# Thirteen full-array products first, and a head's half-column products kept together, in a fused attention and gated-MLP kernel

## The chip, the cores and the metric

The kernel runs on one core of a Trainium2 chip. What counts is the device time of one execution in microseconds (us). Five engines work side by side: TensorE (PE: matrix products, and the loading of their stationary operand, PEld), VectorE (DVE), ScalarE (ACT), GpSimd (POOL), and SyncE (SP), which issues the transfers.

## The reference

Eight batches of eight heads go through attention with a causal mask and a learned decay; the result, with the heads side by side as 512 features, goes through a gated MLP with a spatial product over the 576 tokens. Cut to what matters:

```python
scores = scale * np.matmul(q, k.transpose(0, 1, 3, 2))          # 64 heads, 576 x 576, D = 64
cum = np.cumsum(np.maximum(s, 0.0), axis=-1)
scores = np.where(causal, -1e9, scores + np.minimum(-(cum[..., :, None] - cum[..., None, :]), 0.0))
attn = softmax(scores)
x = (attn @ v) as (batch, 576, 512)

h = gelu(x @ w_in)                                              # 512 -> 1024, tanh form
u, v = h[..., :512], h[..., 512:]
v_n = (v - mean) / sqrt(var + 1e-6) * g_ln
out = x + (u * (w_sg @ v_n + b_sg)) @ w_out                     # w_sg is 576 x 576
```

## The kernel before

All activations lie feature-major. Per head the score matrix is worked in five row tiles (`IT0`, `ITR`, `ITW`): four of 128 query rows, which need 192, 320, 448 and 576 key columns, and one of 64 rows (`it` 0) that needs 64. Scores are products into PSUM (`sc`). DVE adds the mask, takes the row minimum of the negated scores and writes `p`; ACT takes the exponential with its row sum. TensorE transposes `p` block by block into `pt`, and ACT and DVE copy that to `pa`, `pb` and `pd`. Then `pv` forms the weighted sum in the PSUM tile `xx`. The row sums of a pair of heads are transposed once (`pt<-ident,rs`), sent out and read back as a row (`rb`), and POOL multiplies them in.

Three kinds of heads differ in precision. Heads 0 to 11 (`h < NQ`) take their scores from plain fp32 products of `kf` (64 features and one row of the cumulated decay). Heads 0 to 15 (`h < NP`) take the weighted sum in fp32 too. Every other product is a sum of products of rounded halves (fp32r: a high and a low part). One fp32 product is two instructions in the trace, one fp32r product is one.

In fp32 the weighted sum of a head is ten products (`part(side, ...)`): the stationary operand is a block of `v` with 64 columns, and `side` says which 64 of the 128 columns of the array, so which half of `xx`, it goes to. Side 1 sums the output columns 256 to 511, side 0 the others. The last two have 64 rows, since the last 64 keys are a half block.

After every eight heads follows the MLP of a batch: `v_unit` (`vm`), `u_unit` (`um`), `s_unit` (`sm`) and `o_unit` (`om`), all fp32r. Its weights are fetched (`wraw`), taken apart and rounded (`wbits`, `wm`, `wi`, `wo`, `ws`) by ACT, DVE and POOL during the first heads.

The order on each engine isn't that of the code. Each step carries a place in a timetable (`POS`, `spread`), in heads; `SHIFT` moves kinds of instructions by parts of it in five phases, and `plan` lists the instructions by a cost for each and by these priorities. The order it finds is then fixed. The `yield`s in `pv` let other work be placed between the pieces.

At the start the cumulated decay is a product of the decay rows with a triangle of ones (`cps<-tri,sp`), which waits for a transfer and for POOL and DVE, and `WARM` = 2 further products (`wm`) of the same operands follow it, whose result nobody reads. Head 0 has no decay row in `kf` yet, and adds it by products of a single row (`sc<-cf,tri`). Nearly all instructions are recorded at the line of one helper (L404).

Of the kernel before, what the change touches and what calls it, by code (L numbers as in the profile page):

```python
# [9 lines left out]
F32 = mybir.dt.float32  # L10
F32R = mybir.dt.float32r
# [6 lines left out]
B, H, S, D = 8, 8, 576, 64  # L18
# [3 lines left out]
P = 128  # L22
NC = DM // P
NT = 4
REM = S - NT * P
# [10 lines left out]
IT0 = [512, 0, 384, 128, 256]  # L36
COL = [4, 0, 3, 1, 2]
ITR = [64, 128, 128, 128, 128]
# [9 lines left out]
WARM = 2  # L48
FULL = {(128, 192): 300.0, (128, 288): 525.0, (128, 320): 690.0, (128, 448): 830.0, (64, 64): 130.0,
        (64, 128): 150.0, (64, 192): 215.0, (64, 256): 290.0}  # L50
NQ = 12
NP = 16
# [19 lines left out]
MARGIN = 33.09  # L72
# [3 lines left out]
    "act activation p__ 128x192 p__": (0, -1.37, 0, 0, 0),  # L76
    "act activation p__ 128x320 p__": (-2.28, -2.28, -2.28, -2.28, -2.28),
    "act activation p__ 64x64 p__": (2.65, 0, -4.17, 0, 0),
# [3 lines left out]
    "act copy k 128x576 raw": (0, 0, 6.86, 6.86, 6.86),  # L82
    "act copy pah 128x512 pt": (3.74, 3.74, 3.74, 3.74, 3.74),
    "act copy pbh 128x256 pt": (0, 2.82, 1.23, 0, 0),
    "act copy vs 128x384 vr": (0, 0, 0, 5.9, 0),
    "act copy wi 128x256 wbits": (1.22, 1.22, 1.22, 0, 0),
    "act copy wo 128x256 wbits": (0, 0, -0.77, -0.77, 0),
# [8 lines left out]
    "dve scalar_tensor_tensor wbits 128x256 wraw": (0, 0.25, 4.43, 0, 0),  # L96
    "dve scalar_tensor_tensor wm 128x256 wraw": (0, -5.7, 0, 0, 0),
    "dve tensor_copy pbl 128x512 pt": (0, 0, -2.8, 0, 0),
    "dve tensor_copy pdh 128x256 pt": (-3.99, -3.99, -3.99, -3.99, 0),
    "dve tensor_scalar wm 128x256 wbits": (1.21, 1.21, 1.21, 0, 0),  # L100
    "dve tensor_tensor pdh 64x64 pt": (0, 0, 0, 2.01, 2.01),
    "dve tensor_tensor xr 64x64 x": (0, 0, 0, 5.88, 5.88),
    "dve tensor_tensor_reduce p__ 128x192 sc": (-3.17, -3.17, -3.17, -3.17, -3.17),
    "dve tensor_tensor_reduce p__ 128x288 sc": (0, 0.71, 4.68, 0, 0),
    "dve tensor_tensor_reduce p__ 128x320 sc": (4.12, 0.53, 8.43, 1.82, 0),
    "dve tensor_tensor_reduce p__ 64x64 sc": (-9.27, -9.27, -9.27, -9.27, -9.27),
# [18 lines left out]
    "pool tensor_scalar wbits 128x256 wbits": (-4.38, -4.38, -4.38, -4.38, 0),  # L125
    "pool tensor_tensor k 128x576 raw": (0, 0, -8.31, -8.31, -8.31),
    "pool tensor_tensor wo 128x256 wbits": (0, 0, 19.21, 19.21, 0),
    "pool tensor_tensor ws 128x576 wst": (0, 0, -3.49, 0, 0),
# [109 lines left out]
class Program:  # L238
# [14 lines left out]


# [9 lines left out]
    def cost(self, op):  # L264
        e, name, ins, outs, kw = op["eng"].n, op["name"], op["ins"], op["outs"], op["kw"]
        big = [v for v in ins if v.columns() > 1]
        n = outs[0].columns() if outs else big[0].columns()
# [3 lines left out]
        if e == PE:  # L271
            if name == "transpose":
                d, load, port = 110.0, 0.84 * ins[0].columns(), 1.0
            else:
                w, m = ins
                load, n = 0.84 * w.columns(), m.columns()
                d = 0.463 * n if m.dtype == F32R else FULL.get((w.columns(), n), 2.0 * n + 60)
# [116 lines left out]
    def emit(self, tc, first, uses, order, text):  # L394


        real, todo = {}, {}
        for bs in uses:
            for b in bs:
                todo[b] = todo.get(b, 0) + 1  # L400
        for i in text:
            op = self.ops[i]
            f = lambda x: x.make() if isinstance(x, View) else x
            r = getattr(op["eng"].real, op["name"])(*[f(a) for a in op["args"]], **{k: f(v) for k, v in op["kw"].items()})  # L404
            real[i] = r.ins
            for b in uses[i]:
                todo[b] -= 1
                if todo[b] == 0:
                    b.real = None

        tags, same = {}, set()
        for i in text:
            for b in first[i]:
                tags.setdefault(b.tag, []).append(i)
        edges = [(a, b, mybir.DependencyClass.NoSync) for seq in order for a, b in zip(seq, seq[1:])]
        edges += [(a, b, mybir.DependencyClass.NoSync) for seq in tags.values() for a, b in zip(seq, seq[1:])
                  if self.ops[a]["eng"].n != self.ops[b]["eng"].n]
        for a, b, kind in edges:
            tc.add_manual_dep(real[b], real[a].name, mybir.DependencyInfo(kind, mybir.DependencyReason.DATA),
                              reason="order")  # L420
# [129 lines left out]
def tile_attn_gmlp(  # L550
# [45 lines left out]
    def load(h):  # L596
        d = heads[h] = {}
        if h < NQ:
            t = att.tile([P, 2, S], F32, name="kf", tag="k1")
            k, q = d["k"], d["q"] = t[0:D + 1, 0, :], t[0:D + 1, 1, :]  # L600
# [20 lines left out]
    cum = dram.tile([2, BH, S], F32, name="cum")  # L621
    st = moe.tile([P, 5, BH], F32, name="st", tag="vt", bufs=2)
# [21 lines left out]
    wm = ps_m.tile([P, 512], F32, name="wm", tag="m")  # L644
    for i in range(WARM):
        nc.tensor.matmul(wm, sp[:, 0].rearrange("p a h -> p (a h)"), tri[:, 0:512], start=True, stop=True)
# [134 lines left out]
    def qk_part(h, it, pst, c0, j0, j1):  # L781
        d = heads[h]
        i0, r = IT0[it], ITR[it]
# [148 lines left out]
    def pv(h):  # L932
# [20 lines left out]
        if f32:  # L953
            v, pa, pb, pd = d["v"], pt["pa"][0], pt["pb"][0], pt["pd"][0]

            def part(side, c0, c1, w, m, start=False, stop=False):
                nc.tensor.matmul(xx[64 * side:64 * side + 64, c0:c1], w, m, start=start, stop=stop)

            part(1, 256, 512, v[:, 0, :], pa[:, 256:512], start=True)
            part(0, 0, 256, v[:, 0, :], pa[:, 0:256], start=True)  # L960
            yield 0.2
            part(1, 256, 512, v[:, 1, :], pb[:, 512:768])
            part(0, 64, 256, v[:, 1, :], pb[:, 320:512])
            part(1, 256, 448, v[:, 2, :], pb[:, 128:320])
            part(0, 128, 256, v[:, 2, :], pb[:, 0:128])
            yield 0.65
            part(1, 256, 384, v[:, 3, :], pd[:, 192:320])
            part(0, 192, 256, v[:, 3, :], pd[:, 128:192])
            part(1, 256, 320, v[REM:P, 4, :], pd[REM:P, 64:128], stop=True)
            part(0, 256, 320, v[0:REM, 5, :], pd[0:REM, 64:128], stop=True)  # L970
# [237 lines left out]
def _layout(i):  # L1208
# [7 lines left out]
    kf = kq[:NQ].reshape(NQ, 2, D, S).transpose(0, 2, 1, 3)  # L1216
    kf = np.concatenate([kf, np.ones((NQ, 1, 2, S), q.dtype)], axis=1)
    v6 = np.concatenate([v, v[:, NT * P:], v[:, 0:REM], v[:, 0:REM]], axis=1)
    s_t = np.concatenate([i["s"].reshape(BH, S).T, np.zeros((5 * P - S, BH), i["s"].dtype)])
# [36 lines left out]
```

## Time and profile before

| | us |
|---|---|
| median of the runs | 795.68 |
| time of the profiled execution | 795.8 |
| span of its trace | 794.1 |
| TensorE busy | 782.0 (98%) |
| VectorE / ScalarE / GpSimd busy | 599.1 / 562.6 / 488.0 |

The span reaches from the first to the last instruction; 1.7 us of the execution's own time lie around it. The time of the engine that is always busy sets the end; of such an engine one then asks at which pace it works.

### The profile page before, as it was taken

To read this page: it belongs to the slowest core of one execution; us is meant where nothing else is said; L and a number is where in the kernel's file an instruction comes from. 1 tells how busy PE (TensorE), PEld (TensorE's weight loads), DVE (VectorE), ACT (ScalarE), POOL (GpSimd) and SP (SyncE) were. 2 spreads that over 40 slices of the span, in tenths; PEclk is the share of its full clock that TensorE was granted. 3 is DMA by queue.
4 is the path that set the end of the run, shared out by engine and by line. 5 is a ranking of instruction groups with operands and counts; after the bars stand their busy time and mean duration, and the time that the engine had idled before them with its cause. 6 is when DMAs were issued, how large, how long until landed. Compare 5 with 4: busy or idle time off the path is not lost.

```text
span 794.1 us, 16905 instructions
## 1 busy us (share of the span) xinstructions
PE 782.0 (98%) x5271; PEld 692.7 (87%) x5271; DVE 599.1 (75%) x1829; ACT 562.6 (71%) x1550; POOL 488.0 (61%) x762
## 2 busy tenths in 40 slices
PE   7999999999999999999999999999999999999998
PEld 4556667889989999999989999999989999999998
DVE  3477869867699868987799868987689867984562
ACT  2467777866689858987689857987689957972440
POOL 4245779774756766586655856576555856653641
PEclk9999999999999999999999999999999999999999
DMA  6246674545353635356353545355354544411101
GB/s 177 77 113 151 168 205 129 126 103 153 92 144 93 159 104 152 89 141 179 95 133 101 152 119 150 98 133 159 97 133 117 148 134 121 112 33 39 51 7 61
DMA packets 74115, 94.23 MB, mean 119 GB/s; under 512 B 29813, under 2 KB 44597, under 8 KB 74026
## 3 DMA queue, kind: packets, MB, share of 16 engines
q1 hardware_dynamic: 74026, 93.16, 44.4%
q8 instruction: 42, 0.69, 0.4%
q14 instruction: 47, 0.39, 0.2%
HBM read 49.38 MB, written 9.90 MB: 75 GB/s over the span
## 4 chain that ended last, share of the span: by engine, by line
PE 93%; DVE 2%; DMA 2%; ACT 2%; POOL 0%; issue 0%; SPq 0%; ACTq 0%
PE sc L404 16%; PE sm L404 14%; PE om L404 13%; PE um L404 13%; PE xx L404 13%; PE vm L404 12%; PE pt L404 11%; DMA wraw<-in_w_out 1%; ACT p L404 1%; DMA kf<-in_kf 0%; DVE wbits L404 0%; DVE p L404 0%; DMA k<-k 0%; PE cps L404 0%; PE x L404 0%
## 5 line engine op out<-in xcount | busy, mean ns | idle before, releaser
L404 ACT ACTIVATE p<-p,mn 64x64 f32<-64x64 f32 (+4 forms) x320 | 177.8, 556 | 58.9 <-DVE mn L404 56.9
L404 DVE CUSTOM_DVE_ANT_0 p<-sc,mask 128x448 f32<-128x448 f32 (+4 forms) x320 | 123.8, 421 | 24.1 <-PE sc L404 22.6
L404 PE MATMUL sm<-ws,vn 128*128 128x288 f32 x768 | 134.8, 300 | 0.0
L404 PE MATMUL pt<-ident,p 128*128 128x128 f32 x768 | 132.4, 280 | 1.0 <-ACT p L404 0.7
L404 PE MATMUL om<-gt,wo 128*128 128x288 f32 x768 | 129.8, 301 | 0.0
L404 PE MATMUL um<-xs,wi 128*128 128x288 f32 x768 | 127.0, 303 | 0.4 <-DVE vt L404 0.3
L404 PE MATMUL vm<-wi,xs 128*128 128x512 f32 (+1 forms) x416 | 117.6, 404 | 0.0
L404 PEld LDWEIGHTS pt<-ident,p 128*128 128x128 f32 x768 | 93.4, 142 | 23.8 <-issue 11.1
L404 PEld LDWEIGHTS sm<-ws,vn 128*128 128x128 f32 x768 | 112.6, 188 | 1.2 <-issue 0.3
L404 PEld LDWEIGHTS om<-gt,wo 128*128 128x128 f32 x768 | 110.6, 188 | 1.7 <-issue 0.3
L404 PEld LDWEIGHTS um<-xs,wi 128*128 128x128 f32 x768 | 107.6, 188 | 3.3 <-issue 0.8
L404 POOL TENSOR_TENSOR k<-raw,k 128x576 fp32r<-128x576 f32 x52 | 74.7, 1437 | 32.4 <-ACT k L404 30.9
L404 PE MATMUL sc<-k 128*128 128x288 f32 (+4 forms) x312 | 91.2, 304 | 0.0
L404 PE MATMUL sc<-k,q 66*128 66x288 f32 (+4 forms) x312 | 86.8, 307 | 0.0
L404 PEld LDWEIGHTS vm<-wi,xs 128*128 128x128 f32 (+1 forms) x416 | 73.2, 184 | 13.9 <-issue 1.0
L404 POOL TENSOR_SCALAR p<-p 64x64 f32<-64x64 f32 x128 | 30.9, 241 | 81.0 <-ACT p L404 50.5
L404 DVE TENSOR_TENSOR pbl<-pt,pbh 128x512 fp32r<-128x512 f32 x96 | 52.0, 547 | 23.1 <-ACT pbh L404 20.2
L404 POOL TENSOR_TENSOR gt<-u,gt 128x288 fp32r<-128x288 f32 x64 | 50.5, 807 | 22.6 <-ACT gt L404 22.4
L404 DVE SCALAR_TENSOR_TENSOR u<-u,um 128x288 f32<-128x288 f32 x128 | 56.4, 445 | 10.1 <-ACT u L404 9.7
L404 POOL TENSOR_TENSOR xr<-xr,rb 128x576 f32<-128x576 f32 x32 | 45.9, 1434 | 25.8 <-DMA rb<-rd 15.5
L404 POOL TENSOR_TENSOR vs<-vr,vs 128x384 fp32r<-128x384 f32 x48 | 48.7, 1015 | 18.8 <-ACT vs L404 17.7
L404 ACT ACTIVATION_READ_ACCUMULATOR p<-p,mn 128x1 f32 (+1 forms) x320 | 60.0, 188 | 0.0
(129 smaller groups left out, 1702.9 us busy)
## 6 DMA issues: line engine op xcount, KB each, us to landing
k<-k SPq DMA_DIRECT2D x156, 144.0 KB
raw<-in_kq SPq DMA_DIRECT2D x52, 288.0 KB
vr<-in_vp SPq DMA_DIRECT2D x48, 192.0 KB
rb<-rd SPq DMA_DIRECT2D x64, 144.0 KB
out_t<-ot SPq DMA_DIRECT2D x64, 144.0 KB
q<-k SPq DMA_DIRECT2D x52, 144.0 KB
wraw<-in_w_in SPq DMA_DIRECT2D x16, 256.0 KB
kf<-in_kf SPq DMA_DIRECT2D x12, 292.5 KB
```

The costliest lines, as they stand in the source:

```text
L404: r = getattr(op["eng"].real, op["name"])(*[f(a) for a in op["args"]], **{k: f(v) for k, v in op["kw"].items()})
```

## The change

At the start of the program DVE fills a tile `wz` with ones, and 13 products 128x128 by 512 of it (`wm<-wz`, fp32r) come first on TensorE; the two behind `cps` are gone. They wait for that fill alone.

The ten products of a weighted sum become one entry of the plan, a `group`, which is given out as ten products in a row; the two `yield`s stand ahead of it. The last two products take all 128 rows: the host writes zeros into the rows of `v` that don't belong.

The score products of the 64-row tile take 128 columns of queries in heads 0 to 11. The 64 further columns lie behind the queries, so the host lays the queries ahead of the keys; rows 64 to 127 of the result are read by nobody.

`SHIFT` and `MARGIN` have new numbers, so the order is another throughout. The diff, without most of the table:

```diff
-WARM = 2
-FULL = {(128, 192): 300.0, (128, 288): 525.0, (128, 320): 690.0, (128, 448): 830.0, (64, 64): 130.0,
+WARM = 13
+FULL = {(128, 192): 300.0, (128, 288): 525.0, (128, 320): 690.0, (128, 448): 830.0, (64, 64): 130.0, (128, 64): 200.0,
-MARGIN = 33.09
+MARGIN = 57.83
 SHIFT = {
-    "act activation p__ 128x192 p__": (0, -1.37, 0, 0, 0),
+    "act activation p__ 128x192 p__": (2.48, 2.48, 2.48, 2.48, 2.48),
...
+    def group(self, calls):
+        ins = [v for args, _ in calls for v in args[1:]]
+        self.ops.append(dict(eng=self.tensor, name="group", args=calls, kw={}, ins=ins, outs=[args[0] for args, _ in calls],
+                             after=self.gate, key=self.key + self.late))
...
-            k, q = d["k"], d["q"] = t[0:D + 1, 0, :], t[0:D + 1, 1, :]
+            k = d["k"] = t[0:D + 1, 1, :]
+            d["q"] = t[0:D + 1].rearrange("p a n -> p (a n)")
...
+    wz = moe.tile([P, S], F32R, name="wz", tag="xs", bufs=4)
+    nc.vector.memset(wz.bitcast(F32), 1.0)
+    wm = ps_m.tile([P, 512], F32, name="wm", tag="m")
+    for i in range(WARM):
+        nc.tensor.matmul(wm, wz[:, 0:P], wz[:, 0:512], start=True, stop=True)
...
-    wm = ps_m.tile([P, 512], F32, name="wm", tag="m")
-    for i in range(WARM):
-        nc.tensor.matmul(wm, sp[:, 0].rearrange("p a h -> p (a h)"), tri[:, 0:512], start=True, stop=True)
...
-        i0, r = IT0[it], ITR[it]
+        i0, r = IT0[it], P if h < NQ else ITR[it]
...
-            part(1, 256, 512, v[:, 0, :], pa[:, 256:512], start=True)
-            part(0, 0, 256, v[:, 0, :], pa[:, 0:256], start=True)
-            yield 0.2
...
-            part(1, 256, 320, v[REM:P, 4, :], pd[REM:P, 64:128], stop=True)
-            part(0, 256, 320, v[0:REM, 5, :], pd[0:REM, 64:128], stop=True)
+            pieces = [(1, 256, 512, 0, pa[:, 256:512]), (0, 0, 256, 0, pa[:, 0:256]),
+                      (1, 256, 512, 1, pb[:, 512:768]), (0, 64, 256, 1, pb[:, 320:512]),
+                      (1, 256, 448, 2, pb[:, 128:320]), (0, 128, 256, 2, pb[:, 0:128]),
+                      (1, 256, 384, 3, pd[:, 192:320]), (0, 192, 256, 3, pd[:, 128:192]),
+                      (1, 256, 320, 4, pd[:, 64:128]), (0, 256, 320, 5, pd[:, 64:128])]
+            nc.group([((xx[64 * z:64 * z + 64, c0:c1], v[:, j, :], m), dict(start=n < 2, stop=n > 7))
+                      for n, (z, c0, c1, j, m) in enumerate(pieces)])
...
-    kf = kq[:NQ].reshape(NQ, 2, D, S).transpose(0, 2, 1, 3)
+    kf = kq[:NQ].reshape(NQ, 2, D, S)[:, ::-1].transpose(0, 2, 1, 3)
...
+    v6[:NP, NT * P:S] = 0
+    v6[:NP, 5 * P + REM:] = 0
```

What this makes of TensorE's order is seen at two places. The first is the start of the program; before, it is this (`sc<-kf` are head 0's scores, `cps` the cumulated decay):

```order
L404 MATMUL sc<-kf 128x448
L404 MATMUL cps<-tri,sp 128x64 x5
L404 MATMUL cps<-tri,sp 128x512
L404 MATMUL cps<-tri,sp 128x384
L404 MATMUL cps<-tri,sp 128x256
L404 MATMUL cps<-tri,sp 128x128
L404 MATMUL wm<-tri,sp 128x512 x2
L404 MATMUL sc<-kf 128x320
```

On TensorE at the same place, now:

```order
L412 MATMUL wm<-wz 128x512 x13
L412 MATMUL sc<-kf 128x320
L412 MATMUL cps<-tri,sp 128x512
L412 MATMUL cps<-tri,sp 128x384
L412 MATMUL cps<-tri,sp 128x256
L412 MATMUL cps<-tri,sp 128x128
L412 MATMUL cps<-tri,sp 128x64 x5
L412 MATMUL sc<-kf 128x448
```

The thirteen products stand ahead of everything, and nothing else of head 0 has gained a place.

The second is the weighted sum of head 2 (`xx<-pah,vf`, `pbh` and `pdh`), on TensorE. Before, transposes and scores of the next head stand between its pieces:

```order
L404 MATMUL xx<-pah,vf 64x256 x2
L404 MATMUL pt<-ident,p_2_120 128x128
L404 MATMUL pt<-ident,p_4_213 128x128
L404 MATMUL pt<-ident,p_3_122 128x128
L404 MATMUL pt<-ident,p_4_213 128x128
L404 MATMUL sc<-kf 128x288
```

And now, on TensorE:

```order
L412 MATMUL sc<-kf 128x288 x2
L412 MATMUL xx<-pah,vf 64x256 x2
L412 MATMUL xx<-pbh,vf 64x256
L412 MATMUL xx<-pbh,vf 64x192 x2
L412 MATMUL xx<-pbh,vf 64x128
L412 MATMUL xx<-pdh,vf 64x128
L412 MATMUL xx<-pdh,vf 64x64 x3
L412 MATMUL sc<-kf 128x448
L412 MATMUL sc<-kf 128x64
```

All ten pieces now stand behind the last scores of the next head, and the narrow score (now 128x64, before 64x64) follows the wide one directly. Over the whole program TensorE's order has 54 separate stretches of such pieces before, and 16 now, one for each of heads 0 to 15.

## Rows read from the trace of the kernel before

**Rows 1.** The page's first line: the span.

```profile
span 794.1 us, 16905 instructions
```

**Rows 2.** Busy time by stretch: PE, PEld, DVE, ACT, POOL, then granted clock and DMA.

```profile
4.87:35.50 30.63, 30.63 (x76) 16.21 (x78) 11.70 (x41) 11.25 (x34) 9.53 (x15) 1.00 0.45 128
...
70.00:140.00 70.00, 67.06 (x419) 45.86 (x416) 57.10 (x175) 51.28 (x153) 54.70 (x79) 1.00 0.64 170
...
200.00:780.00 580.00, 579.19 (x4065) 546.52 (x4065) 456.23 (x1371) 432.00 (x1164) 360.19 (x567) 1.00 0.43 112
```

**Rows 3.** TensorE in order of time, the first 33 us (start, us, instruction).

```profile
4.87 1.85 PE L404 MATMUL sc<-kf 64*128 64x448 f32 x2 [4.87 <-DMA kf<-in_kf]
6.65 2.77 PE L404 MATMUL cps<-tri,sp 128*128 128x64 f32 x9
9.22 1.16 PE L404 MATMUL wm<-tri,sp 128*128 128x512 f32 x2
10.32 2.39 PE L404 MATMUL sc<-kf 64*128 64x320 f32 x4
...
31.64 1.12 PE L404 MATMUL xx<-pbh,vf 128*64 128x256 f32 x2
32.68 0.90 PE L404 MATMUL pt<-ident,p 128*128 128x128 f32 x3
```

**Rows 4.** The same view around the weighted sum of head 2.

```profile
45.91 0.65 PE L404 MATMUL xx<-pah,vf 128*64 128x256 f32 x4
46.49 0.66 PE L404 MATMUL pt<-ident,p 128*128 128x128 f32 x4
...
47.56 0.65 PE L404 MATMUL xx<-pbh,vf 128*64 128x256 f32 x2
48.14 0.55 PE L404 MATMUL pt<-ident,p 128*128 128x128 f32 x3
...
49.01 0.38 PE L404 MATMUL pt<-ident,p 128*128 128x128 f32 x2
49.33 0.54 PE L404 MATMUL xx<-pbh,vf 128*64 128x192 f32 x2
49.80 0.33 PE L404 MATMUL pt<-ident,p 128*128 128x128 f32 x1
50.05 0.54 PE L404 MATMUL xx<-pbh,vf 128*64 128x192 f32 x4
...
51.00 1.02 PE L404 MATMUL sc<-kf 65*128 65x448 f32 x2
51.86 0.38 PE L404 MATMUL pt<-ident,p 128*128 128x128 f32 x2
```

**Rows 5.** The same view, transposes between full-array products.

```profile
177.31 0.82 PE L404 MATMUL pt<-ident,p 128*128 128x128 f32 x6
177.89 0.38 PE L404 MATMUL om<-gt,wo 128*128 128x288 f32 x1
```

**Rows 6.** DVE in order of time, its first work.

```profile
0.89 0.17 DVE L404 MEMSET ident<- 128x128 f32 x1 [0.89 <-PEq L1243]
...
1.66 1.14 DVE L404 MEMSET q<- 2x576 f32 x2 [0.16 <-issue]
```

**Rows 7.** TensorE in order of time, a weighted sum in two stretches.

```profile
99.76 0.65 PE L404 MATMUL xx<-pal,vf 128*64 128x256 f32 x4
100.34 0.50 PE L404 MATMUL vm<-wi,xs 128*128 128x512 f32 x1
100.77 0.81 PE L404 MATMUL xx<-pbl,vf 128*64 128x256 f32 x7
...
102.16 0.33 PE L404 MATMUL pt<-ident,p 128*128 128x128 f32 x1
```

**Rows 8.** Groups by form of stationary loads, 36 to 100 us (busy us, mean ns).

```profile
L404 PEld LDWEIGHTS sc<-kf 65*128 65x128 f32 x90 | 14.5, 191 | 3.6 <-DVE mn L404 1.0 <-issue 0.9
...
L404 PEld LDWEIGHTS sc<-kf 65*64 65x64 f32 x18 | 1.7, 135 | 3.0 <-issue 3.0
```

More of the change, by code (lines that the diff above doesn't have):

```diff
@@ L75 @@
 SHIFT = {
-    "act activation p__ 128x192 p__": (0, -1.37, 0, 0, 0),
-    "act activation p__ 128x320 p__": (-2.28, -2.28, -2.28, -2.28, -2.28),
-    "act activation p__ 64x64 p__": (2.65, 0, -4.17, 0, 0),
[3 rows of a table removed]
[L82 to L87, printed above, removed]
[8 rows of a table removed]
@@ L96 @@
[L96 to L103, printed above, removed]
@@ L104 @@
-    "dve tensor_tensor_reduce p__ 128x288 sc": (0, 0.71, 4.68, 0, 0),
-    "dve tensor_tensor_reduce p__ 128x320 sc": (4.12, 0.53, 8.43, 1.82, 0),
-    "dve tensor_tensor_reduce p__ 64x64 sc": (-9.27, -9.27, -9.27, -9.27, -9.27),
[18 rows of a table removed]
[L125 to L128, printed above, removed]
[6 rows of a table removed]
+    "act activation p__ 128x192 p__": (2.48, 2.48, 2.48, 2.48, 2.48),
@@ new lines @@
+    "act activation p__ 128x320 p__": (-5.18, -5.18, -5.18, -5.18, -5.18),
+    "act activation p__ 128x448 p__": (0, 0, 2.82, 0, 0),
+    "act activation p__ 128x576 p__": (0, 0, 1.09, -2.07, 0),
+    "act activation p__ 64x64 p__": (-3.38, -3.38, -3.38, -3.38, -3.38),
+    "act activation u 128x288 um": (0, 0, 0, 1.31, 0),
+    "act activation vt 128x512 vt": (0, 0, 1.52, 1.52, 1.52),
+    "act activation wbits 128x256 wraw": (1.26, 1.26, 1.26, 1.26, 0),
+    "act copy k 128x576 raw": (0, 0, 4.79, 4.79, 4.79),
@@ new lines @@
+    "act copy pah 128x512 pt": (0, -6.06, 0, 3.13, 0),
+    "act copy pbh 128x256 pt": (0, 3.91, 0, 0, 0),
+    "act copy pdh 128x256 pt": (0, 0, 0, -3.4, -3.4),
+    "act copy vs 128x384 vr": (0, 0, 0, 3.81, 3.81),
+    "act copy wo 128x256 wbits": (0, 0, 0.9, 0.9, 0),
[4 rows of a table added]
+    "dve scalar_tensor_tensor wbits 128x256 wraw": (0, 1.42, 5.63, 0, 0),
+    "dve tensor_copy pbh 128x512 pt": (3.79, 3.79, 3.79, 3.79, 0),
+    "dve tensor_tensor pal 128x512 pt": (0, 0, 0, 2.09, 2.09),
+    "dve tensor_tensor xr 64x64 x": (0, 0, 0, 7.1, 7.1),
@@ new lines @@
+    "dve tensor_tensor_reduce p__ 128x192 sc": (0, 0, 0, -3.43, -2.62),
+    "dve tensor_tensor_reduce p__ 128x288 sc": (0, 1.64, 0, 0, 0),
+    "dve tensor_tensor_reduce p__ 128x320 sc": (0, 5.94, 7.42, 4.73, 0),
+    "dve tensor_tensor_reduce p__ 128x448 sc": (3.92, 3.92, 3.92, 3.92, 3.92),
+    "dve tensor_tensor_reduce p__ 64x64 sc": (-22.23, -22.23, -22.23, -22.23, -22.23),
[21 rows of a table added]
+    "pool tensor_scalar wbits 128x256 wbits": (-3.46, -3.46, -3.46, -3.46, 0),
+    "pool tensor_tensor bs 128x1 bs": (0, 0, 0, -2.56, 0),
@@ L135 @@
+    "pool tensor_tensor k 128x576 raw": (0, 0, 0, -8.27, 0),
+    "pool tensor_tensor wi 128x256 wbits": (0.15, 0.15, 0.15, 0, 0),
+    "pool tensor_tensor wo 128x256 wbits": (0, 0, 13.78, 13.78, 0),
+    "pool tensor_tensor ws 128x576 wst": (0, 0, -0.44, 0, 0),
[4 rows of a table added]
 }
@@ L271, in cost @@
         if e == PE:
-            if name == "transpose":
+            if name == "group":
+                d, load = 2150.0, 54.0
+            elif name == "transpose":
                 d, load, port = 110.0, 0.84 * ins[0].columns(), 1.0
@@ L403, in emit @@
             f = lambda x: x.make() if isinstance(x, View) else x
-            r = getattr(op["eng"].real, op["name"])(*[f(a) for a in op["args"]], **{k: f(v) for k, v in op["kw"].items()})
-            real[i] = r.ins
+            calls = op["args"] if op["name"] == "group" else [(op["args"], op["kw"])]
+            name = "matmul" if op["name"] == "group" else op["name"]
+            real[i] = [getattr(op["eng"].real, name)(*[f(a) for a in args], **{k: f(v) for k, v in kw.items()}).ins
+                       for args, kw in calls]
             for b in uses[i]:
@@ L417, in emit @@
                   if self.ops[a]["eng"].n != self.ops[b]["eng"].n]
+        edges = [(real[a][-1], real[b][0], kind) for a, b, kind in edges]
+        edges += [(a, b, mybir.DependencyClass.NoSync) for rs in real.values() for a, b in zip(rs, rs[1:])]
         for a, b, kind in edges:
-            tc.add_manual_dep(real[b], real[a].name, mybir.DependencyInfo(kind, mybir.DependencyReason.DATA),
+            tc.add_manual_dep(b, a.name, mybir.DependencyInfo(kind, mybir.DependencyReason.DATA),
                               reason="order")
@@ L953, in pv @@
         if f32:
+            yield 0.2
+            yield 0.65
             v, pa, pb, pd = d["v"], pt["pa"][0], pt["pb"][0], pt["pd"][0]
-            def part(side, c0, c1, w, m, start=False, stop=False):
-                nc.tensor.matmul(xx[64 * side:64 * side + 64, c0:c1], w, m, start=start, stop=stop)
-            part(1, 256, 512, v[:, 0, :], pa[:, 256:512], start=True)
-            part(0, 0, 256, v[:, 0, :], pa[:, 0:256], start=True)
-            yield 0.2
[L962 to L968, printed above, removed]
-            part(1, 256, 320, v[REM:P, 4, :], pd[REM:P, 64:128], stop=True)
-            part(0, 256, 320, v[0:REM, 5, :], pd[0:REM, 64:128], stop=True)
+            pieces = [(1, 256, 512, 0, pa[:, 256:512]), (0, 0, 256, 0, pa[:, 0:256]),
[5 more added lines that the diff above has]
+                      for n, (z, c0, c1, j, m) in enumerate(pieces)])
             nc.scalar.copy(out=xt[hs, 0:256], in_=xx[0:64, 0:256])
```

64 rows, old and new, of the table SHIFT are left out of this document.

## The prediction

> **What bounds the kernel now.** I read the busy times by stretch first, then TensorE in order of time, comparing the same shapes early and late. The span is 794.1 us [rows 1]; TensorE is busy 579.19 us of the 580 between 200 and 780 us, and all 30.63 us of the stretch from 4.87 to 35.5 us [rows 2]. There is no second bound to look for: time that TensorE saves comes off the end, unless it starts to wait for something that is now hidden. It waits for others only between 70 and 140 us, where it is busy 67.06 of 70 us and DVE 57.10.
>
> A busy TensorE can still work at half pace, and here it does. Head 0's first score (448 columns, two instructions) goes from 4.87 to 6.65 us, so 1.78 us [rows 3]; the same shape in head 4 goes from 51.00 to 51.86, so 0.86 us [rows 4]. A lone pair of half-column pieces takes 1.04 us at 31.64 [rows 3] and 0.58 us at 47.56 [rows 4]. The granted clock is printed as 1.00 in all stretches [rows 2], but durations a factor 1.8 to 2.07 apart are what its two levels, 1.2 and 2.4 GHz, would give. I take it that the clock was at the lower level until about 35.5 us, between the slow shapes of 31.64 and the quick ones of 45.91, and that the printed clock doesn't show it; the reader is to trust the starts of equal shapes.
>
> **The change, part by part.** The sum is made against the profiled execution's own 795.8 us (span 794.1 and 1.7 around it), which stands 0.1 above the median of 795.68.
>
> *The thirteen products.* They wait for one DVE fill of 576 columns. DVE starts at 0.89, and two fills of 576 columns take 1.14 us [rows 6], so TensorE can start at about 1.5 us. It now starts at 4.87, when `kf` lands [rows 3]. Two such products in the old place go from 9.22 to 10.32, 0.55 us each, with the change to a 64-row product behind them in it [rows 3]; without that I take 0.45 (estimate; half of it if the clock rises among them). Thirteen are 5.9 us (7.2 at 0.55), to about 7.4 us. The fill moves DVE's other first work by 0.6 us, which lies under them: nothing.
>
> If they bring the clock up, the work of the old stretch from 4.87 runs at full level. 30.63 us divided by 2.07 are 14.8, by 1.8 are 17.0; I take 15.5, since most of it is wide. Of this go 0.55 for the two old `wm`, and 0.8 for head 0's pieces and the first narrow scores (below): 14.1. From 7.4 that ends at 21.5. But what hid behind slow products shows: head 0's scores go through DVE, ACT and back to the transposes before TensorE has other work, and in the stretch DVE has 11.70 us to do and ACT 11.25 [rows 2], in 14.1 instead of 30.63. For this I add 2.0 us (0 to 4). So 23.5 instead of 35.5: **-12.0 us** (-9 to -14).
>
> *The block of ten pieces.* Head 2 has four stretches: 45.91 to 46.49, 47.56 to 48.14, 49.33 to 49.80 and 50.05 to 51.00, together 2.58 us [rows 4]. Entering one costs too: two transposes ahead of one take 0.32 us [rows 4], six ahead of a full-array product 0.58, so 0.097 each [rows 5]; with the slower first one allowed for, an entry costs 0.09. So 2.58 + 4 x 0.09 = 2.94 us. A head with two stretches takes 0.58 + 1.39 + 2 x 0.09 = 2.15 [rows 7]. Heads 1 to 15 have 50 stretches, 3.33 each, so by the line between the two about 2.68. One stretch needs the 1.97 of the two, less one leaving (some 0.05) and the change to 64 rows inside (some 0.09, as an entry), plus one entry: 1.92; I take 2.05, because in one go the loads of 64 columns have less to hide behind. 15 x 0.63 = **-9.4 us** (-7 to -11).
>
> The price is order: the block can't start until the last copy (`pd`) is done, and whole heads of it stand ahead of the next transposes. In the order now, the next head's last two 288-column scores stand just before it; they cover that copy.
>
> *The narrow score.* In heads 1 to 11 it saves one entry and part of one leaving, 0.09 + 0.05. Its two loads grow from 135 to 191 ns [rows 8], 0.11 together if nothing hides them. Net between 0.03 and 0.2; I take 0.1: **-1.1 us** (0 to -2.2).
>
> *New waits.* From head 2 until the MLP fills in, TensorE has only the head chains. About 10% less of its work makes DVE's 57.10 of 70 [rows 2] 57.10 of 63, so 0.91, with ACT and POOL near 0.85. Engines work that densely later too, but there TensorE has an MLP to turn to. It lost 2.94 us in that stretch before; I add **+3 us** (0 to 8). The weights' preparation lies on these engines and is what would be late next.
>
> *The new order elsewhere.* I counted changes between stationary shapes in both orders: 148 against 151 in the fp32r work, 59 against 62 around the row-sum transposes. Six at 0.09: **+0.5 us**. From 200 us on TensorE is full whatever the order.
>
> Sum: -12.0 - 9.4 - 1.1 + 3 + 0.5 = -19.0, so **776.8 us**; with the bounds of the terms, some 770 to 783.
>
> **The rivals.**
>
> *The clock comes up late all the same.* For it: the products from 6.65 to 10.32, nine `cps` and two `wm`, are nearly all of the same full-array kind [rows 3], and didn't bring it up; 13 are more, but no row shows that they suffice. Then it might rise where it did before, near the end of head 0's pieces. The start loses 1.4 us (2.5 later, less 1.1 for the old two) and saves about as much by head 0's own pieces, so the first term is nil and the time is 776.8 + 12 = 788.8.
>
> *The slowness isn't the clock at all.* The Trainium skill, "TensorE: Matmul & The Clock Gate", section "Why this matters for your kernels", has it that TensorE reaches full clock by working without gaps. By that rule the old stretch should have risen long before 35.5, and something else would be slow in it. This trace disagrees: 30.63 of 30.63 us busy and still 1.78 us for what later takes 0.86. As a mechanism of this kernel: first operands slow to arrive, say. Then the first term is +1.4 instead of -12, so 790.2.
>
> *The other engines take over.* If DVE and ACT can't follow, TensorE waits 10 us instead of 3: 784. For it speaks that all three come near one load; against it, that only 2.94 us were lost in the densest stretch.
>
> *Slower: the clock falls back.* Place: right after the thirteen products, at head 0's single-row and 64-row products, or in the waits of about a microsecond behind them. While it is down, work that takes 1 us takes 2. A head is about 6.5 us of TensorE's work at full level. The break-even against 795.8 lies at 19 us of such work, three heads; six heads cost 39, so 815. Against it: the heads from 3 to the MLP have the same narrow products, and the wide score at 51.00 is as quick as they come. The same page of the Trainium skill, section "Part 4: PE-mode transpose", holds that transposes don't engage the full clock. Here they run at 0.097 us each at 177.31 and the heads full of them keep the full level [rows 4, 5], so I give that little.
>
> **How the numbers follow.** Chances: forecast 0.62, clock late 0.16, other engines 0.12, not the clock 0.04, fallback 0.05; 0.01 is left. The time is the forecast's, 776.8. Its own span of 770 to 783 holds most of its 0.62; the range goes on to 789 to take in the other engines and nearly all of the late clock, which makes some 0.85 of the chance. 2% is about what a measurement of this kernel can tell from no change: below 779.9 is faster. Some 0.85 of the forecast's chance lies there: 0.53, and a little of the rest: 0.55. Slower by over 2%, above 811.6, is most of the fallback: 0.04. The rest, 0.41, is within.
>
> **What would show it.** In the profile after: `wm` starting near 1.5 us and ending near 7; the first 448-column score pair of head 0 in about 0.9 us, not 1.78; head 4's wide score at about 37.5 us, not 51.00; 16 stretches of half-column pieces, each about 2.0 us; TensorE's idle time before 140 us not above 10. I am wrong if the early shapes are still slow behind the thirteen products, if the blocks take as long as the pieces did (2.6 us), or if TensorE waits for DVE, ACT or a `kf` transfer in most heads.

## The result, and the profile after

The changed kernel takes 776.48 us in the median (775.45 to 777.15), the kernel before 797.0 in the runs beside it; the ratio is 0.9747 with an interval of 0.9719 to 0.9774. Ratios here leave disturbed executions out, of which the kernel before had more than the changed one, so its medians wander between 796 and 802 us and the ratios are the better measure. The prediction said 776.8 us and faster by over 2%. Its number is right; of the terms behind it, the one for the start is far too large and the one for the block too small.

The page after, its first lines (beside [rows 1] and the table of before):

```profile
span 773.7 us, 16912 instructions
...
PE 763.5 (99%) x5282; PEld 696.2 (90%) x5282; DVE 591.9 (77%) x1830; ACT 556.7 (72%) x1550; POOL 487.7 (63%) x762
```

The span is 20.4 us shorter, TensorE's busy time 18.5. It is still the engine that is always busy. Busy time by stretch (columns as in [rows 2]):

```profile
0.00:4.87 4.87, 3.30 (x8) 2.62 (x9) 3.55 (x11) 1.28 (x1) 4.06 (x15) 1.00 0.60 141
4.87:35.50 30.63, 30.63 (x123) 20.21 (x122) 16.25 (x60) 15.45 (x48) 11.10 (x17) 0.72 0.52 146
35.50:70.00 34.50, 33.40 (x235) 24.12 (x233) 30.03 (x110) 28.46 (x94) 19.76 (x31) 1.00 0.56 153
70.00:140.00 70.00, 66.38 (x476) 54.28 (x473) 58.07 (x183) 56.20 (x163) 61.65 (x90) 1.00 0.65 168
140.00:180.00 40.00, 39.57 (x304) 37.12 (x303) 26.65 (x88) 27.56 (x79) 26.83 (x36) 1.00 0.48 126
180.00:760.00 580.00, 579.63 (x4074) 547.48 (x4072) 453.92 (x1375) 426.12 (x1165) 361.17 (x572) 1.00 0.42 113
```

The second row is the surprise: in the stretch that should now be quick, the mean granted clock is 0.72. Finer stretches of the same view:

```profile
7.37:14.08 6.71, 6.71 (x29) 4.04 (x29) 1.58 (x6) 3.12 (x8) 2.87 (x3) 1.00 0.79 271
14.08:18.00 3.92, 3.92 (x9) 1.65 (x8) 1.85 (x8) 1.81 (x9) 2.05 (x4) 0.50 0.44 85
18.00:23.50 5.50, 5.50 (x20) 4.18 (x19) 4.14 (x14) 2.66 (x7) 1.69 (x3) 0.50 0.46 139
23.50:31.20 7.70, 7.70 (x34) 5.68 (x33) 4.56 (x16) 4.39 (x16) 1.86 (x4) 0.50 0.31 89
```

The clock was at full after the thirteen products, until 14.08 us, then at half until 31.15, though TensorE was busy without a gap. (1.00 is printed also for the time up to 7.25, the first recorded change. The thirteen products lie there and take 5.8 us, 0.45 each; eight products of that size at 196.91 take 2.11 us, 0.26 each. Ahead of the first recorded change, the view shows 1.00 whatever the level. That is why the 1.00 of before up to 35.5 [rows 2] was wrong.) TensorE in order of time shows the same in the work itself, to be held against [rows 3, 4]:

```profile
1.57 5.87 PE L412 MATMUL wm<-wz 128*128 128x512 f32 x13 [1.57 <-DVE wz L412]
7.37 0.80 PE L412 MATMUL sc<-kf 64*128 64x320 f32 x2
...
13.11 0.59 PE L412 MATMUL sc<-kf 64*128 64x192 f32 x2
13.63 1.55 PE L412 MATMUL sc<-cf,tri 1*128 1x192 f32 x4
15.11 1.32 PE L412 MATMUL sc<-kf 64*128 64x288 f32 x2
16.37 1.32 PE L412 MATMUL sc<-cf,tri 1*128 1x288 f32 x2
...
25.81 1.12 PE L412 MATMUL xx<-pah,vf 128*64 128x256 f32 x4
...
28.99 1.54 PE L412 MATMUL pt<-ident,p 128*128 128x128 f32 x6
...
31.50 1.08 PE L412 MATMUL sc<-kf 65*128 65x448 f32 x4
...
40.40 0.65 PE L412 MATMUL xx<-pah,vf 128*64 128x256 f32 x4
...
42.06 1.19 PE L412 MATMUL sc<-kf 65*128 65x448 f32 x4
...
196.91 2.11 PE L412 MATMUL vm<-wi,xs 128*128 128x512 f32 x8
```

The thirteen run from 1.57 to 7.37, as predicted (1.5 to 7.4). From 15.11 a pair of 288 columns takes 1.26 us, as it did at 19.41 before (the next entry begins at 20.67): low pace. Head 0's block takes 3.18 us (25.81 to 28.99), head 2's 1.66 (40.40 to 42.06); before, head 2's pieces took 2.58 in four stretches with an entry to each [rows 4]. Head 4's wide score starts at 42.06, not at the 37.5 of the prediction.

### The profile page after: what moved, and what is told of

The parts are those of the page before. It is cut to its first block, busy times and chain, and to the rows that moved or that the text cites. A ratio compares the mean times of both kernels' runs of the same rounds, so it can differ in the third digit from the quotient of the medians.

```text
span 773.7 us, 16912 instructions
## 1 busy us (share of the span) xinstructions
PE 763.5 (99%) x5282; PEld 696.2 (90%) x5282; DVE 591.9 (77%) x1830; ACT 556.7 (72%) x1550; POOL 487.7 (63%) x762
## 4 chain that ended last, share of the span: by engine, by line
PE 88%; DMA 3%; DVE 3%; POOL 3%; ACT 1%; SPq 1%; issue 1%; ACTq 0%; DVEq 0%; POOLq 0%
PE sm L412 15%; PE sc L412 14%; PE om L412 13%; PE vm L412 12%; PE um L412 12%; PE pt L412 11%; PE xx L412 10%; SPq L412 1%; DVE p L412 1%; PE wm L412 1%; DMA q<-k 1%; POOL wbits L412 1%; DMA wraw<-in_w_out 1%; DMA raw<-in_kq 1%; POOL ws L412 1%
## 5 line engine op out<-in xcount | busy, mean ns | idle before, releaser
L412 ACT ACTIVATE p<-p,mn 128x320 f32<-128x320 f32 (+4 forms) x320 | 178.4, 559 | 26.5 <-DVE mn L412 22.1
L412 DVE CUSTOM_DVE_ANT_0 p<-sc,mask 128x320 f32<-128x320 f32 (+4 forms) x320 | 126.9, 421 | 14.1 <-PE sc L412 7.9
L412 PE MATMUL pt<-ident,p 128*128 128x128 f32 x768 | 130.7, 280 | 4.7 <-DVE rt L412 1.2
L412 PE MATMUL sm<-ws,vn 128*128 128x288 f32 x768 | 126.9, 300 | 0.0
L412 PE MATMUL om<-gt,wo 128*128 128x288 f32 x768 | 121.3, 299 | 0.0
L412 PE MATMUL um<-xs,wi 128*128 128x288 f32 x768 | 120.6, 299 | 0.0
L412 PEld LDWEIGHTS sm<-ws,vn 128*128 128x128 f32 x768 | 109.3, 188 | 0.2
L412 PEld LDWEIGHTS om<-gt,wo 128*128 128x128 f32 x768 | 107.5, 188 | 0.9
L412 PE MATMUL sc<-k,q 66*128 66x288 f32 (+4 forms) x312 | 84.6, 309 | 0.0
L412 PEld LDWEIGHTS sc<-k 128*128 128x128 f32 (+1 forms) x312 | 55.9, 181 | 2.7
```

The lines of the kernel that those rows point to most:

```text
L412: real[i] = [getattr(op["eng"].real, name)(*[f(a) for a in args], **{k: f(v) for k, v in kw.items()}).ins for args, kw in calls]
```

## The experiments

**The order.** The table of shifts (`SHIFT`) shapes the order. The first two runs exchange the table, and take the block apart under the new one. `old_table` is the changed kernel with

```diff
-MARGIN = 57.83
+MARGIN = 33.09
 SHIFT = {
...
```

and the rows of the kernel before.

> The changed kernel with the table of shifts and the margin of the kernel before; all else as changed. If the order found anew is worth little, since TensorE is full from 180 us on: 775 to 779 us. Rival (the new order holds the gain, by fewer waits between 35 and 140 us): TensorE's idle time there grows from 4.7 us to 8 or more, 780 us or more.

It took 797.51 us (794.83 to 802.33), a ratio of 1.0014 (0.9996 to 1.0031) to the kernel before: the whole gain is gone. Its stretches:

```profile
35.50:70.00 34.50, 30.96 (x192) 22.07 (x191) 21.89 (x85) 22.68 (x74) 15.69 (x23) 0.90 0.43 112
70.00:140.00 70.00, 61.43 (x357) 45.42 (x355) 52.20 (x166) 48.49 (x141) 53.39 (x73) 0.90 0.60 160
```

TensorE is idle for 3.5 + 8.6 us here, against 1.1 + 3.6 in the changed kernel, and a mean clock of 0.90 means 20 us at half. That is 7.4 + 10 of the 21.4 us by which its span is the longer (795.1 against 773.7). DVE is busy less than after (74.1 against 88.1 us), and so is ACT: no engine is overloaded. What TensorE waits for, in the whole program (total, times, longest):

```profile
PE sc L413 <- DMA kf<-cf: 2.8, 2, 2.6
PE sc L413 <- DVE mn L413: 2.0, 4, 1.1
PE pt L413 <- ACT p L413: 1.8, 3, 0.8
```

The longest wait is for a transfer, the decay row of a head, and ends at 100.84, ahead of the fall at 102.17; most of the others are for steps of the chain from score to transpose. The rival was right, and stronger than I wrote it.

`pieces_apart` is the changed kernel with its own table and this:

```diff
...
+            part(1, 256, 512, 0, pa[:, 256:512], start=True)
+            part(0, 0, 256, 0, pa[:, 0:256], start=True)
             yield 0.2
...
-            nc.group([((xx[64 * z:64 * z + 64, c0:c1], v[:, j, :], m), dict(start=n < 2, stop=n > 7))
-                      for n, (z, c0, c1, j, m) in enumerate(pieces)])
```

> The changed kernel with the ten pieces of a weighted sum as separate entries of the plan again, with its two interruptions, but all of 128 rows; the table of shifts is that of the changed kernel. In the changed kernel a block takes 1.67 us where the pieces of a head took 2.35 in the mean, plus an entry for each stretch. Theory A (the block gives 0.9 us a head in 15 heads, mostly entries and lone halves): 776.5 + 14 less 1.4 for the rows that stay 128 = about 789 us, with 45 to 55 stretches. Theory B (the block is worth the 0.63 us a head of the prediction): 785 us. Rival: it is worth little and the gain is the start's: below 779 us.

795.57 us (792.01 to 797.37). That is theory A and more, but a table that fits blocks was given pieces, so it doesn't price the block. The next run comes nearer to that.

**One part alone, in an order held fixed.** `before_block` plans the kernel before as it was, and then moves pieces in TensorE's finished list only:

```diff
     _, _, _, seqs = plan(cost, pre, new, uses, order, bufs, prio, after)
...
+    for ns in pieces.values():
+        for last in reversed(ns):
+            pe = [n for n in seqs[PE] if n not in ns or n == last]
+            at = pe.index(last)
+            pe[at:at + 1] = ns
...
```

> The kernel before, planned as it was; then only the pieces of a head's weighted sum (heads 0 to 15) are moved in TensorE's finished order to the place of the last of them, and all other instructions of all engines keep their order. The last two pieces keep 64 rows. Theory A (the block itself is worth what the traces of before and after show, 0.92 us a head less 0.09 for the 64 rows, in 15 heads): 12.5 us less, about 783 us, as long as TensorE finds no new waits where the moved pieces used to fill in. Theory B (without an order made for it the block gives nothing, since TensorE then waits for the copies): idle time between 35 and 140 us above 10 us and 793 us or more.

794.51 us, ratio 0.9969 (0.9938 to 0.9999). Both theories hold a part. A block in its trace goes from 46.79 to 48.60, 1.81 us, so the work did get shorter:

```profile
46.79 0.65 PE L404 MATMUL xx<-pah,vf 128*64 128x256 f32 x4
47.27 0.76 PE L404 MATMUL xx<-pbh,vf 128*64 128x256 f32 x7
47.83 0.22 PE L404 MATMUL xx<-pdh,vf 128*64 128x64 f32 x1
47.87 0.33 PE L404 MATMUL xx<-pbh,vf 128*64 128x192 f32 x1
47.88 0.79 PE L404 MATMUL xx<-pdh,vf 128*64 128x64 f32 x7
48.60 0.64 PE L404 MATMUL sc<-kf 65*128 65x448 f32 x1
```

And the time saved came back as waits:

```profile
35.50:70.00 34.50, 31.72 (x204) 21.06 (x202) 24.74 (x95) 24.70 (x83) 16.36 (x26) 1.00 0.45 122
70.00:140.00 70.00, 63.14 (x398) 45.01 (x396) 52.27 (x162) 47.77 (x138) 51.52 (x72) 0.95 0.61 160
```

9.6 us of idle TensorE instead of 2.9 [rows 2], and a new stretch at half clock of 6.8 us (0.05 of 70, doubled), which costs 3.4. With 2.1 us more idle behind 140 us, that is about the 12.5 us of theory A. This profiled execution is the slowest of the ten, though (798.2). The four with a mean granted clock of 1.00 took 791.74 to 794.13, so the clock doesn't fall in all of them, and where it holds, the block in the old order gives some 5 us.

So a block in the old order (794.51) and pieces under the new table (795.57) each give little or nothing, and so does the block under the old table (797.51). Only the block together with an order fitted to it gives 776.48.

`before_warm` does the same for the thirteen products: first on TensorE, the two old ones out, all else in the order of before.

```diff
+    seqs[DVE].insert(0, p0)
+    seqs[PE][0:0] = range(p0 + 1, p0 + 1 + len(fresh) - 1)
```

> The kernel before, planned as it was; then only the thirteen products of a tile of ones are put first on TensorE and the two old ones taken out, all else in the same order. Theory A (as in the changed kernel they buy some 7 us at full clock, then it falls back): they begin 3 us earlier, end 2.5 us after the old first score, and 6.8 us of work are quick: about 793 to 795 us. Theory B (the prediction's term of 12 us): 784 us.

793.72 us, ratio 0.995 (0.9911 to 0.999). Theory A: in its trace the clock is full from 6.20 to 13.02, then low until 33.50. `no_warm` asks it the other way round, in the changed kernel, with the order of all else kept:

```diff
-WARM = 13
+WARM = 0
```

> The changed kernel without the thirteen products (their fill stays). Theory A (they gave full clock from 7.3 to 14.1 us only, 6.8 us of work, and cost 2.5 us of later start): the early shapes are slow from 4.9 us until a block or so of half-column pieces, 776.5 + 6.8 - 2.5 = 780.8 us. Theory B (they are worth the 12 us that the prediction gave to the start): 788 us. If they are worth nothing: 774 us.

778.08 us (776.07 to 779.04): the thirteen products are worth 1.6 us here, less than both theories gave, and the two kernels' ranges overlap. Without them the clock rises once, at 31.75, and head 2's wide score starts at 33.50 instead of 31.50.

**Why the clock falls.** `h0_128rows` gives head 0's score and decay products 128 rows, and leaves all else of the changed kernel but its order, which is planned anew:

```diff
+                nc.gpsimd.memset(t[D:P], 0.0)
+                nc.sync.dma_start(out=t[0:D], in_=kf[h][0:D])
...
-            nc.tensor.matmul(o, one[:, 0:r], cf[0:1, j0:j1], start=False, stop=True)
+            nc.tensor.matmul(o, sel[:, 0:r], cf[:, j0:j1], start=False, stop=True)
```

> The changed kernel with one more change: head 0's score products take 128 rows instead of 64 (rows 64 to 127 are zeros), and its decay comes from a product of 128 rows (a stationary tile whose first row is ones) instead of a single row; the result is the same. In the changed kernel the shapes were quick from 7.4 us, slow again from 14.1 to 31.2 us. Theory A (the clock falls back because of head 0's narrow-row products): the slow stretch of 17.1 us does not come, or comes later and shorter; 8.5 us less, so about 768 us; 772 if it is halved. Theory B (it falls back after the thirteen products whatever follows): slow again at about 14 us, and 776.5 us as in the changed kernel.

772.74 us (771.27 to 775.21). The long slow stretch is gone; one of 3.4 us comes from 23.43 to 26.85. TensorE's row ahead of it:

```profile
18.00:23.50 5.50, 3.12 (x19) 1.66 (x19) 4.20 (x17) 5.06 (x17) 2.35 (x5) 0.99 0.42 113
```

Here it was idle for 2.4 of 5.5 us, waiting for ACT (its longest wait is 1.7 us, a transpose for the copy `pbh`). So 6.8 of the 8.5 us were won on the clock, and some 3 given back in waits behind head 0's softmax, which come with this kernel's own order.

`decay_128` gives 128 rows to the decay alone (the single row and zeros below it); head 0's own scores keep 64.

> The changed kernel with head 0's decay products of 128 rows instead of one (a stationary tile whose first row is ones); its score products keep their 64 rows. Theory A (the single rows let the clock fall at 14.1 us): no slow stretch there, as in h0_128rows, 772 to 774 us. Theory B (the 64-row products do, or both together): slow again from about 14 us on, 776 us.

769.29 us (766.67 to 771.2), a ratio of 0.9624 (0.9552 to 0.9695), the best of all kernels here and below the time that either theory gave. The clock rises at 7.71 and stays. By its trace the order of every engine is that of the changed kernel, but for three fills more on DVE, so nothing but the rows differs. Without the single-row products the clock doesn't fall, though the 64-row ones between them are as they were. Whether single rows would do it beside products of 128 rows, no run asks. Two of its stretches, the first beginning where the changed kernel fell:

```profile
14.08:18.00 3.92, 3.49 (x17) 2.06 (x17) 3.12 (x13) 3.14 (x12) 2.42 (x5) 1.00 0.59 150
...
23.50:31.20 7.70, 7.20 (x53) 5.48 (x52) 6.65 (x24) 6.58 (x25) 5.10 (x9) 1.00 0.54 139
```

and its TensorE in order of time, where head 2's wide score stands at 24.40, not 31.50:

```profile
21.27 0.65 PE L412 MATMUL xx<-pah,vf 128*64 128x256 f32 x4
...
22.93 0.88 PE L412 MATMUL pt<-ident,p 128*128 128x128 f32 x6
...
24.40 1.08 PE L412 MATMUL sc<-kf 65*128 65x448 f32 x4
```

It is 7.2 us below the changed kernel, and 7.1 of these are won by that score already. 17.07 us at half pace would be 8.5; 1.1 us of it comes back as idle TensorE between 4.87 and 35.5. What brings the clock back is open: in the changed kernel it rose at 31.15, 13.5 us after the last single-row product (16.37 to 17.62), with TensorE busy all the while, and `decay_128` runs the same work without a fall.

`h0_no_warm` takes the thirteen products out of `h0_128rows`, in that kernel's order.

```diff
+    seqs = [[at[n] for n in seq if n not in gone] for seq in seqs]
```

> The kernel h0_128rows in its own order, without the thirteen products and their fill. Theory A (head 0's products over 128 rows bring the clock up by themselves, soon after 4.9 us): 771 to 774 us, as with them. Theory B (the thirteen are what brings it up, and the 128 rows only hold it): slow until a block of half-column pieces at 25 to 31 us, 781 us or more.

774.1 us (772.59 to 775.4). Theory A: head 0's work over 128 rows brings the clock up itself, at 14.58 us instead of 6.37, and the thirteen add 1.4 us, within the scatter of the two.

**The small parts**, in the changed kernel's own order. `narrow_64`:

```diff
+            op["args"], op["outs"], op["ins"] = (o[0:64], w[:, 0:64], m), [o[0:64]], [w[:, 0:64], m]
```

> The changed kernel in its own order, with the score of the 64-row tile of 64 columns again in heads 0 to 11. By the two traces an fp32 narrow score with what it does to its neighbours takes 0.35 us with 64 columns and 0.17 with 128: 11 heads, 2.0 us more, 778.5 us. By the prediction's 0.1 us a head: 777.6 us. If the clock hangs on it, the slow stretch from 14 to 31 us grows, 780 us or more.

776.37 us (775.22 to 777.43), the same as the changed kernel. `rows_64`:

```diff
+                calls[n] = ((o, w[rows], m[rows]), kw)
```

> The changed kernel in its own order, with the last two pieces of each block of 64 rows again. In before_block the blocks, whose last pieces have 64 rows, take 1.81 us, in the changed kernel 1.67: 15 heads times 0.15 are 2.2 us more, 778.7 us. If the spare 0.15 us is lost in waits of TensorE anyway: 776.5 us.

775.51 us (774.64 to 775.62), also no slower, though its blocks take 1.81 us instead of 1.67 (39.81 to 41.62 in its trace). Neither is worth a measurable part of the gain. Where the 2 us went that each should have cost isn't shown: TensorE's idle time between 35.5 and 180 us is 5.1 us in `narrow_64`, as in the changed kernel, and 4.4 in `rows_64`.

**No table.** `before_plain` and `after_plain`, both with a margin of 45 besides:

```diff
-SHIFT = {
...
+SHIFT = {}
```

> The changed kernel with an empty table of shifts and a margin of 45, so with an order that nobody fitted. Theory A (the gain needs an order fitted to the blocks): above 790 us, with TensorE idle for 8 us or more between 35 and 140 us. Theory B (only a foreign table hurts, as in old_table): 776 to 784 us.

> The kernel before with an empty table and the same margin of 45. Theory A (both kernels lose alike without a fitted order, and the change itself is worth some 12 to 20 us between two unfitted orders as well): 805 us or more, some 15 us above after_plain. Theory B (before's pieces, which the plan can place one by one, fill its waits, and it hardly needs the table): 796 to 800 us, within 8 us of after_plain.

833.86 us for `after_plain` and 848.85 for `before_plain`, two runs each. Theory A in the main: both lose, and the change is worth 15 us between two orders that nobody fitted (11 to 19 by the single runs). TensorE of `after_plain` is idle for 8.3 us between 35.5 and 140, as I wrote, but that was the small part. In the stretch that is full in both fitted kernels, TensorE of the plain ones, before and then after, is

```profile
180.00:760.00 580.00, 555.98 (x3718) 511.06 (x3717) 431.11 (x1333) 417.41 (x1143) 340.01 (x528) 0.98 0.43 116
```

```profile
180.00:760.00 580.00, 556.43 (x3732) 511.57 (x3731) 434.08 (x1335) 417.47 (x1143) 338.62 (x527) 0.99 0.42 113
```

idle for 24 us in either. In the whole program some 26 us of the 57 that each span gains are idle TensorE; the rest isn't taken apart. The fit of the table matters over the whole program, and more than the change.

## Why the prediction was right

**The bound, and the hidden half pace: right.** Equal shapes at two paces meant the lower level, and the trace after records such a stretch (0.50) at the pace that I read it from.

**The thirteen products, -12.0 us: wrong, the term that failed.** Their own part went as written (1.57 to 7.37, clock up at 7.25). What failed is "the work of the old stretch runs at full level". It held to 14.08, then came the rival "the clock falls back", at a place that I named, head 0's single-row products (`decay_128`), for 17.07 us. By my own sign (early shapes still slow behind the thirteen products) this part was wrong. I had given that rival 0.05 and priced it as the end on the slow side, with the clock away for heads. It came back at 31.15, 2.2 us behind head 0's block. What the products are worth is 1.6 us (`no_warm`), or 3.7 in the order of before (`before_warm`). The -12 was there to be had: `decay_128` has its head-2 score at 24.40. Before, it stood 11.9 us later, about as the sum had it:

```profile
36.27 1.02 PE L404 MATMUL sc<-kf 65*128 65x448 f32 x2
```

**The block, -9.4 us: right in kind, too small.** I took 2.05 us; it is 1.67. A lone half costs as much as a pair: before, one product on one side took 0.58 us (47.56 to 48.14) and two on the two sides took 0.58 as well (45.91 to 46.49) [rows 4]. In one go the two sides overlap all along, and the loads of 64 columns, for which I had added 0.13 us, cost nothing that shows. My 0.05 us for leaving a stretch stood on no row. With one entry the block is 1.76 against the 2.68 that I had estimated, 0.92 in 15 heads: 13.8 us of TensorE's work, and 1.5 or so of head 0's at low pace. No single run shows these as time saved: the block pays only in an order fitted to it. The narrow score, -1.1, isn't measurable.

**The new waits, +3 us: right in size.** 5.1 us of idle TensorE between 35.5 and 180 (1.1 + 3.6 + 0.4) against 2.9 before, all of it between 70 and 140 [rows 2], so +2.2.

**The order, +0.5 us: the term that I understood least.** I counted its entries, and took waits as a property of the work. `old_table` and `before_block` show that the same products with another order wait 7 us more and lose the clock besides; in `old_table` that is some 17 of the 21 us. "Other engines take over" was my name for it, at 784 us; it isn't their load (DVE did less per us in `old_table`), it is the order in which the steps of the chain stand.

So the sum came out within 0.4 us since some 9 us too much at the start met about 4 too little in the block, one or so in the waits, and a rest of a few us that no run separates: the head-2 score is 4.8 us earlier, the rest of the program 15.6 us shorter, and the block less the waits explains about 12 of these. That the errors cancel so closely is luck. Had the clock held as the prediction had it, the time would have been near the 769.29 us of `decay_128`, just below the range that begins at 770.

## What to carry to other kernels

Compare equal shapes early and late before believing a clock column, and look at what stands right behind a warm-up: products of a single row in otherwise dense work can undo it. Filling the rows with zeros cost TensorE nothing here: the pair of 448 columns took 0.94 us with one row (10.85 to 11.79) and with 128 (11.04 to 11.98 in `decay_128`). Pieces that each use half of the array belong together; but where TensorE is full and the order is fitted, time taken out of it was worth little until the order was fitted again. A part is priced only with the order held fixed, and even then only for that order. An idle stretch can cost twice, where the clock falls behind it.

## What the hardware showed that I had not expected

The clock fell while TensorE was busy 6.71 of 6.71 us, with products of a single row among those of 64 rows; with 128 rows in their place, and the 64-row ones left, it stayed at full for the whole program. In `h0_128rows` it fell behind a stretch with 3.12 of 5.50 us busy; that the idle time made it fall is argued from where it stands, no run changes it alone. Two chains of half-column products in one go take 1.67 us a head, 0.15 less than when the last two have 64 rows.
